# Reordering the first loads of an attention and MLP kernel: x tile 1 moves to the SP queue ahead of the keys, and wq moves behind the Exp warm-up on ACT

## Chip, cores, metric

One core of a Trainium2 chip. The metric is the device time of one execution in microseconds (us). A profile is one execution of its kernel, and its span is about 1.8 us shorter than the measured time of the same execution.

## The reference, cut to what matters

```python
x = A_x                                  # 2048 x 512, bf16
xn = _layernorm(x, axis=-1)
q = heads(xn @ wq)                       # 32 heads of 128
p = softmax(einsum("bhqd,bhkd->bhqk", q, k_cache) * 128 ** -0.5)
s = (p @ v_cache, heads side by side) @ wo
g = silu(relu(xn @ w1 + b1) ** 2 @ w2 + b2)
return x + s * g
```

(Condensed.) The projections start from xn, so no query and no score can be computed before the first tile of x is in SBUF.

## The kernel before

It is tuned: 4 query blocks of 512 rows, 32 heads each, with TensorE (PE) fed without a gap once it runs. Only the start matters here. Block 0 is brought in as four x tiles of 128 rows ("tile 0" to "tile 3"). Head 0's keys come in two halves and are transposed on PE. In the traces each engine works its list in program order (PE before the change: keys 4.86, tile 0 at 5.71, keys 5.95, projection 6.72 us). The loads are issued as below (SP and ACT each have a queue; a load without an engine goes to SP):

```python
    ln_load(0, 0, SP)          # x tile 0
    ln_load(0, 1, AC)          # x tile 1, on ACT's queue
    load_k0(0)                 # head 0's keys, first half
    fill_wq(0, AC)             # head 0's columns of wq, on ACT's queue
    load_k0(1)                 # head 0's keys, second half
    E(AC, partial(_act, out=th_t[:, 0, 0:1], in_=warm[:, 0:1], func=ACT.Exp), deps=[t_warm])
    ln_load(0, 2, SP)
    ln_load(0, 3, SP)
    fill_wq(1)
    load_v0(0)
    load_v0(1)
    # ... cut ...
```

And the work that waits for them, in the order in which PE and VectorE (DVE) get it:

```python
    warm_up(36)                # 36 dummy products, to bring PE to full clock (products 107 ns apart, then 56)
    k0_transpose(0)            # PE: keys, first half     (needs the load of that half)
    k0_copy(0)                 # ACT
    ln_bn(0, 0)                # DVE: statistics of tile 0
    ln_rstd(0, 0, eng=DV)      # DVE, GpSimd
    ln_bn(0, 1)                # DVE: statistics of tile 1 -- ahead of the next line on DVE
    ln_scale(0, 0)             # DVE: xn of tile 0
    first_transpose(0)         # PE
    k0_transpose(1)            # PE: keys, second half
    k0_copy(1)                 # ACT
    # ... cut ...
    first_copy(0)              # DVE
    first_proj(0)              # PE: head 0's queries of tile 0 (needs wq)
    # ... cut ...
    first_evac(0)
    first_transpose(1)
    gen_scores(0)              # PE: "the first scores"
```

The softmax here doesn't subtract the row's maximum and nothing guards it: scores larger than these inputs give would overflow.

## Time and profile before

| | before |
|---|---|
| time | 1238.17 us median of 3 runs (1237.9 to 1238.31) |
| PE busy | 99% of the span of 1236.1 us |
| tile 0 landed | 3.43 us |
| first projection starts on PE | 6.72 us |
| first scores start on PE | 7.58 us |

A load counts as landed when the last of its 16 semaphore increments is recorded. Those times come from the trace's records of increments, and the other two from the chain of waits, whose columns are start, length and what it was. The prediction shows that chain up to the projection. Here is the line after it:

```profile
7.58 1.05 PE psA L157 x16
```

From here on PE (TensorE) works without a gap worth the name.

### The profile page before, as it was taken

What the parts mean: (1) busy time and instruction counts of PE and PEld (TensorE: products, weight loads), DVE (VectorE), ACT (ScalarE), POOL (GpSimd) and SP (SyncE); (2) the same over time, 40 slices, a digit from 0 to 9 for tenths busy, and PEclk for the clock granted to TensorE, in tenths of its full rate; (3) what the DMA queues carried; (4) which work ended last, traced back from release to release, by engine and by line L of the source; (5) the groups of instructions that cost most, each with busy time, mean ns of one, the idle gap of its engine ahead of it and who ended that gap; (6) DMA issues with size and microseconds to landing.
All of it is one profiled execution on the core that took longest, in us unless ns stands there. A gap on an engine that the chain in (4) does not pass through costs nothing.

```text
span 1236.1 us, 26728 instructions
## 1 busy us (share of the span) xinstructions
PE 1220.8 (99%) x11678; PEld 819.1 (66%) x11885; DVE 472.8 (38%) x953; ACT 1054.6 (85%) x1044; POOL 32.0 (3%) x73
## 2 busy tenths in 40 slices
PE   9999999999999999999999999999999999999998
PEld 7666666666666666666666666666666666666665
DVE  4453323244435332334444532333344333324333
ACT  7888888888888888888888888888888888888885
POOL 1010000000002000000000200000000000000000
PEclk9999999999999999999999999999999999999999
DMA  9999998787879897768779878787778788878771
GB/s 211 203 245 194 187 178 134 130 144 143 140 152 171 144 158 129 141 138 144 133 135 169 171 138 144 141 148 133 134 146 148 146 154 158 137 134 146 145 124 31
DMA packets 686868, 185.41 MB, mean 150 GB/s; under 512 B 673536, under 2 KB 685568, under 8 KB 686752
## 3 DMA queue, kind: packets, MB, share of 16 engines
q1 hardware_dynamic: 684656, 179.62, 80.0%
q0 software_dynamic: 1424, 3.81, 1.2%
q8 instruction: 94, 1.54, 0.6%
q10 hardware_dynamic: 672, 0.26, 0.1%
q14 instruction: 22, 0.18, 0.0%
HBM read 96.60 MB, written 2.10 MB: 80 GB/s over the span
## 4 chain that ended last, share of the span: by engine, by line
PE 98%; issue 1%; DVE 0%; DMA 0%; POOL 0%; DVEq 0%
PE psO L157 38%; PE psA L152 35%; PE psF L152 25%; PE psA L157 0%; DMA x_ln<-in_A_x_dram 0%; DVE out_t L165 0%; PE psF L196 0%; DVE tmp_t L175 0%; PE psO L152 0%; DVE xnT L179 0%; DVE st_t L200 0%; POOL rstd L165 0%; DVE xn_t L171 0%; DVE mv_t L204 0%; DVE ve_t L171 0%
## 5 line engine op out<-in xcount | busy, mean ns | idle before, releaser
L161 ACT ACTIVATE pT<-psA 128x1024 bf16<-128x1024 f32 x1024 | 1044.5, 1024 | 162.9 <-PE psA L152 117.6
L157 PEld LDWEIGHTS psO<-v_sb,pT 128*128 128x128 bf16 x8192 | 547.9, 98 | 240.3 <-issue 12.4
L157 PE MATMUL psO<-v_sb,pT 128*128 128x129 bf16 x8192 | 631.2, 220 | 0.5
L152 PE MATMUL psA<-qt_sb,kT 128*128 128x512 bf16 x1840 | 562.9, 379 | 10.1
L179 DVE COPY o_un<-psO 128x258 f32<-128x258 f32 x256 | 97.4, 422 | 399.5 <-PE psO L157 398.8
L152 PE MATMUL psF<-xnT,wq_sb 128*128 128x512 bf16 (+1 forms) x508 | 165.7, 374 | 0.4 <-DVE xnT L179 0.2
L152 PE MATMUL psF<-wo_all,oT 128*128 128x512 bf16 x478 | 163.2, 379 | 0.1
L152 PEld LDWEIGHTS psA<-qt_sb,kT 128*128 128x128 bf16 x2032 | 157.0, 98 | 0.0
L179 DVE CAST qt_sb<-psF 128x512 bf16<-128x512 f32 (+1 forms) x130 | 88.0, 677 | 97.3 <-PE psF L152 93.7
L165 DVE TENSOR_TENSOR o_bf<-o_un,rden 128x512 bf16<-128x512 f32 x128 | 88.6, 692 | 4.7 <-DVE rden L183 0.3
L152 PEld LDWEIGHTS psF<-xnT,wq_sb 128*128 128x128 bf16 x520 | 50.3, 98 | 60.0 <-issue 0.3
L171 DVE TENSOR_SCALAR r_t<-psF,b1f 128x512 bf16<-128x512 f32 x56 | 42.0, 750 | 117.4 <-PE psF L152 117.4
L152 PEld LDWEIGHTS psF<-wo_all,oT 128*128 128x128 bf16 x480 | 46.9, 98 | 56.4
L152 PE MATMUL psF<-xnT,w_sb 128*128 128x512 bf16 x224 | 77.1, 379 | 0.0
L152 PE MATMUL psF<-w_sb,h2T 128*128 128x512 bf16 x223 | 73.7, 379 | 0.0
L152 PEld LDWEIGHTS psF<-xnT,w_sb 128*128 128x128 bf16 x224 | 21.9, 98 | 26.4
L152 PEld LDWEIGHTS psF<-w_sb,h2T 128*128 128x128 bf16 x224 | 21.9, 98 | 26.4
L165 DVE TENSOR_TENSOR z_t<-psF,b2bc 128x512 f32<-128x512 f32 x16 | 11.1, 692 | 67.2 <-PE psF L152 62.0
L165 DVE TENSOR_TENSOR acc<-psF,acc 128x512 f32<-128x512 f32 x28 | 19.3, 689 | 30.0 <-PE psF L152 30.0
L208 POOL DMA_DIRECT2D out_dram<-out_t x12 | 6.7, 554 | 891.1 <-DVE out_t L165 891.1
L165 DVE TENSOR_TENSOR h2T<-r_t 128x512 bf16<-128x512 bf16 x56 | 23.8, 426 | 1.9
L183 DVE RECIPROCAL rden<-o_un 128x4 f32<-128x4 f32 x128 | 22.9, 179 | 4.4
(47 smaller groups left out, 165.2 us busy)
## 6 DMA issues: line engine op xcount, KB each, us to landing
v_sb<-in_A_v_cache_dram SPq DMA_DIRECT2D x127, 512.0 KB, 4.7
wq_sb<-in_A_wq_dram SPq DMA_DIRECT2D x127, 128.0 KB, 3.1
wo_all<-in_A_wo_dram SPq DMA_DIRECT2D x4, 1024.0 KB, 6.4
w_sb<-in_B_w_dram SPq DMA_DIRECT2D x14, 256.0 KB, 4.1
oT<-o_bf SPq DMA_TRANSPOSE x128, 4.0
x_t<-in_A_x_dram POOLq DMA_DIRECT2D x16, 128.0 KB, 3.5
kT<-in_A_k_cache_dram SPq DMA_TRANSPOSE x127, 4.5
x_ln<-in_A_x_dram SPq DMA_DIRECT2D x15, 128.0 KB, 4.0
```

What stands on the lines that cost most here:

```text
L152: return e.matmul(out, lhsT, rhs, start=start, stop=stop)
L157: return e.matmul(out, lhsT, rhs, start=start, stop=stop, skip_group_check=True)
L161: return e.activation(out, in_, func, bias=bias, scale=scale)
L165: return e.tensor_tensor(out, in0, in1, op)
L171: return e.tensor_scalar(out, in0, scalar1=scalar1, scalar2=scalar2, op0=op0, op1=op1)
L179: return e.tensor_copy(out, in_)
L183: return e.reciprocal(out, in_)
L208: return e.dma_start(out, in_)
```

## The change

The intent: tile 0 should have the DMA engines to itself, since layernorm of tile 0 is at the head of the chain. So tile 1 stands behind it on SP, the keys behind both, and wq is alone on ACT's queue, behind Exp.

```diff
     ln_load(0, 0, SP)
-    ln_load(0, 1, AC)
+    ln_load(0, 1, SP)
     load_k0(0)
-    fill_wq(0, AC)
     load_k0(1)
     E(AC, partial(_act, out=th_t[:, 0, 0:1], in_=warm[:, 0:1], func=ACT.Exp), deps=[t_warm])
+    fill_wq(0, AC)
     ln_load(0, 2, SP)
```

## The prediction

> **What bounds the kernel now.** I read the page first (busy shares and the chain that ended last), then busy time by stage, then the chain of waits over the first 10 us, then the timeline of the same stretch with the DMA issues, and last the recorded increments of each load's semaphore. The page:
>
> ```profile
> span 1236.1 us, 26728 instructions
> PE 1220.8 (99%) x11678; PEld 819.1 (66%) x11885; DVE 472.8 (38%) x953; ACT 1054.6 (85%) x1044; POOL 32.0 (3%) x73
> ...
> PE 98%; issue 1%; DVE 0%; DMA 0%; POOL 0%; DVEq 0%
> ```
>
> TensorE (PE) is busy 99% of the span and is 98% of the chain that ended last. The change touches no instruction on PE; it reorders the loads at the start. So it can win only what PE loses there. Busy time by stage:
>
> ```profile
> 0.00:5.00 5.00, 4.02 (x38) 3.90 (x39) 1.48 (x4) 1.49 (x2) 1.83 (x12) 1.00 0.63 177
> 5.00:10.00 5.00, 4.61 (x70) 3.84 (x68) 4.06 (x14) 3.77 (x4) 2.20 (x5) 1.00 1.25 260
> 10.00:20.00 10.00, 9.87 (x140) 8.21 (x139) 3.83 (x13) 8.22 (x10) 1.34 (x3) 1.00 1.03 202
> ```
>
> The columns are stretch and length, then busy us on PE, PEld, DVE, ACT, POOL, then clock, DMA share and GB/s. From 10 us on PE is dense. The 4.02 us of PE work in the first stretch are the 36 dummy matmuls that warm it up, not real work, so the first real product waits on the chain that fills the first 7.6 us:
>
> ```profile
> 0.72 2.71 DMA x_ln<-in_A_x_dram
> ...
> 3.45 0.71 DVE st_t L200
> ...
> 4.64 0.58 POOL rstd L165
> ...
> 5.25 0.42 DVE xn_t L171
> ...
> 5.71 0.41 PE psF L196 x4
> ...
> 6.15 0.44 DVE xnT L179
> ...
> 6.72 0.38 PE psF L152 x4
> ```
>
> This is layernorm of x tile 0, its transpose on PE at 5.71, the copy, and head 0's first projection at 6.72. The chain starts with the landing of tile 0: issued at 0.72, landed at 3.43. From landing to the PE transpose is 5.71 - 3.43 = 2.28 us of fixed work on DVE and POOL. The loads and the transposes of head 0's keys stand around it:
>
> ```profile
> 0.72 0.41 ACTq L208 DMA_DIRECT2D x_ln<-in_A_x_dram  x1
> 0.72 0.40 SPq L208 DMA_DIRECT2D x_ln<-in_A_x_dram  x1
> ...
> 1.16 0.46 ACTq L208 DMA_DIRECT2D wq_sb<-in_A_wq_dram  x1
> 1.18 0.89 SPq L208 DMA_DIRECT2D kT<-in_A_k_cache_dram  x2
> ...
> 1.65 1.28 ACT L161 ACT_TABLE_LOAD   x1 [1.65 <-PEq L1024]
> ...
> 4.86 0.73 PE L196 MATMUL psO<-ident,kT 128*128 128x128 bf16 x8
> ...
> 5.89 0.49 PEld L196 LDWEIGHTS psO<-ident,kT 128*128 128x128 bf16 x8
> ```
>
> The semaphore records say when each landed: tile 0 3.43, tile 1 3.60, first half of the keys 4.82, head 0's wq 5.19, second half of the keys 5.85, tiles 2 and 3 at 6.23 and 6.64, head 1's wq 7.24, the two halves of the values 8.44 and 9.51. PE takes its work in program order: keys half one (4.86, 0.04 us after its landing, and just after the last dummy matmul at 4.69), x tile 0's transpose, keys half two (5.89, 0.04 us after its landing), first projection. Three things therefore stand within 0.3 us of one another on PE: tile 0 and the two halves of the keys.
>
> **What the Trainium skill says.** "DMA: Bandwidth & Descriptors", section "Issuing engines are not separate DMA queues": loads from SP and ACT end on the same 16 DMA engines and interleave; a second issuer saves issue time only. The trace agrees: both x tiles are issued at 0.72 and land 0.17 us apart. Same page, "Queues, rings and completion order": within one engine descriptors of one ring start in order, and an engine alternates between rings packet by packet. The trace agrees: from 2.4 to 2.6 us, 34 packets of SP's ring and 26 of ACT's began, and no key packet (behind tile 0 on SP's ring) before 2.6. "Advanced Engine Details and Errata", section "Sequencer Loop": engine instructions are pushed into a queue, and the sequencer goes on to control instructions. If it holds for a DMA issue behind an ACTIVATE, wq is issued at once; no record of the kernel before shows that order on ACT. "ScalarE: Activation LUTs", section "What ACT_TABLE_LOAD costs", gives about 1283 ns for a table load; the trace has 1.28 us.
>
> **The change part by part.** It adds and removes no instruction; it moves two DMA issues.
>
> 1. Tile 1 moves from ACT's ring to SP's, behind tile 0. Tile 0 then has the DMA engines to itself until something else comes on ACT's ring. A 1 KB packet took 46 ns (median), and a tile has 128 over 16 engines, so tile 1 is 8 x 46 = 0.37 us of each engine, mostly interleaved with tile 0 now. Part of the stretch up to 2.4 us is slow start, which stays. I expect tile 0 to land 0.2 to 0.35 us earlier, about 3.15. Tile 1 is second, so it lands near where it did (both are the first 256 KB in either order), about 3.6; DVE wants it only at 4.47, or 4.2 when shifted.
>
> 2. SP has one more issue (0.40 us plus a 0.06 us gap) ahead of the keys, so all its later issues come 0.46 us later. Keys half one is issued at 1.64 instead of 1.18. But it was not waiting for its issue: it was issued at 1.18 and its first packet ran at 2.6, and from 2.4 us on the DMA engines are about 90% busy. The same bytes (both tiles, wq, keys) lie ahead of each landing as before, only reordered, so I estimate 4.7 to 4.95 for half one and 5.8 to 6.0 for half two. Later landings gain up to 0.46 us, against slacks of 1 us or more: head 1's wq 7.24 for use at 8.64, values 9.51 for use at 11.52, and head 1's keys 12.75 for use at about 15.7. Nothing new there.
>
> 3. wq now stands behind the Exp warm-up on ACT. If the sequencer passes the queued Exp, it issues at about 0.8 to 1.0; if it waits for the table load and the Exp (1.28 + 0.21 us after about 0.75), at about 2.3. With the 4.0 us it took from issue to landing it is there at about 5.0 or 6.3, for a projection at 6.69 now and about 6.5 after. Early, its 256 B packets (18 ns each, 32 per engine, 0.58 us) compete with tile 0 and take some of point 1 back: eight alternations cost tile 0 up to 8 x 18 = 0.14 us. Late, they compete with the keys.
>
> The sum on PE: keys half one can start no earlier than about 4.78 (end of the dummies), takes eight issues in 0.57 us and ends at 5.35 to 5.55. Tile 0's transpose is ready at 3.15 + 2.28 = 5.43, so it starts at about 5.45 to 5.6 instead of 5.71. Keys half two (0.50 us) follows its landing: 5.85 + 0.04 + 0.50 = 6.39 at best, against xnT ready at 5.5 + 0.98 = 6.48. So the first projection starts at about 6.5 instead of 6.69. The gain is 0.1 to 0.3 us, I take 0.2, and PE carries it to the end as it is dense from there. 1238.17 - 0.2 = 1237.97, say 1238.0. In per cent it is 0.02, below the spread of the three runs of before (0.41 us).
>
> **The rivals.** (a) Keys take the place of tile 0: half one is issued 0.46 us later and lands that much later, at 5.28; then its transposes end at 5.9 and tile 0's transpose starts 0.15 to 0.2 us later than before. For it: PE was released by that landing at 4.86, with no slack. Against it: busy DMA engines from 2.4 us. It would make 1238.3 to 1238.5. (b) wq becomes the last to come: issued behind table load and Exp, landing after 6.7. For it: 4.0 us to landing; against it: its ring would be free, while before it stood behind tile 1. 0 to 0.3 us lost, so up to 1238.5. (c) The full intent: tile 0 0.4 us earlier and the keys unharmed, 1237.8. PE's own order and the second half of the keys stand against more. (d) Anything of 2% (25 us) would need PE to stop in the body, where the order of loads is untouched and SP waits for PE anyway. I see no way.
>
> **Range and chances.** All cases lie within 0.5 us of 1238.0; the runs of before spread over 0.4 us, and another build or another hour may add as much. So 1237.3 to 1238.8. Within 2% is all but certain.
>
> **What would show it.** In the changed trace: tile 0's landing near 3.15 with DVE's first statistics right behind; the keys' first landing below 4.95; the transpose of x tile 0 at 5.45 to 5.6; head 0's first projection near 6.5; and the same dense PE after that. A wq issue on ACT at 0.8 to 1.0 or at about 2.3 decides point 3. The prediction is wrong if the first projection starts later than 6.7, or if PE's idle after 10 us changes by more than some tenths of a us.

## More of the kernel before

I read each increment as the share of one of the core's 16 DMA engines. That is an assumption: the records show 16 increments per load and do not name the engine.

## The result, and the profile after

The changed kernel took 1238.44 us (median of 6, 1238.1 to 1239.05) against 1238.02 us (6 runs, 1237.9 to 1238.31). The ratio is 1.0004, interval 0.9991 to 1.0017: the same. Executions over 1.5% slower than the fastest of the same kernel are left out of the means. Ratios here are over the same rounds; they agree with the ratio of the mean times within 0.0001. In means, the changed kernel is 0.46 us slower (1238.51 against 1238.05). That is inside the reported interval (a second set of rounds, no. 2, gave 0.48 again), but the trace can say where it came from. The page of the changed kernel:

```profile
span 1236.5 us, 26935 instructions
PE 1231.8 (100%) x11885; PEld 819.3 (66%) x11885; DVE 472.3 (38%) x953; ACT 1053.7 (85%) x1044; POOL 32.0 (3%) x73
...
PE 99%; DMA 0%; DVE 0%; SPq 0%; issue 0%; DVEq 0%
```

PE busy seems to rise by 11 us. It did not: before, the page counted 11678 products beside 11885 weight loads, so 207 records of products were missing; after, none is. PEld, with all its records, has 819.1 and 819.3 us.

Busy time by stage (columns as in the prediction: stretch, length, busy PE, PEld, DVE, ACT, POOL, clock, DMA share, GB/s):

```profile
0.00:5.00 5.00, 4.02 (x36) 3.76 (x36) 1.77 (x5) 1.49 (x2) 2.04 (x12) 1.00 0.61 173
5.00:10.00 5.00, 4.32 (x63) 3.83 (x63) 3.28 (x12) 3.43 (x4) 1.98 (x4) 1.00 1.07 219
10.00:20.00 10.00, 9.93 (x145) 8.44 (x143) 3.90 (x12) 8.30 (x9) 1.34 (x3) 1.00 1.04 198
```

From 0 to 5 us PE lost its two key transposes (38 products before, 36 now); from 5 to 10 us the DMA rate fell from 260 to 219 GB/s and PE did 63 products in place of 70. The chain of waits at the start is another one now:

```profile
2.11 4.50 DMA kT<-in_A_k_cache_dram
...
6.66 0.62 PE psO L196 x8
7.28 0.24 PE psF L152 x4
...
7.98 1.05 PE psA L157 x16
```

It no longer begins with tile 0. It begins with the second half of the keys, issued at 2.11 and landed at 6.61 (ahead of it the view has only SP's three earlier issues, from 0.72). PE transposes it at 6.66, then projects, and the first scores start at 7.98, not 7.58: 0.40 us later, and the span is 0.4 us longer. The timeline of the same stretch (start, length, engine, line, operation):

```profile
0.72 1.28 ACT L161 ACT_TABLE_LOAD   x1 [0.72 <-PEq L1024]
0.72 0.87 SPq L208 DMA_DIRECT2D x_ln<-in_A_x_dram  x2
...
0.96 0.41 ACTq L208 DMA_DIRECT2D wq_sb<-in_A_wq_dram  x1
...
1.65 0.90 SPq L208 DMA_DIRECT2D kT<-in_A_k_cache_dram  x2
...
3.08 0.69 DVE L200 BATCH_NORM_STATS2 st_t<-x_ln 128x6 f32<-128x512 bf16 x1 [3.08 <-DMA x_ln<-in_A_x_dram]
...
5.96 0.40 PE L196 MATMUL psF<-ident,xn_t 128*128 128x128 bf16 x4
```

Tile 0 is in at 3.05 and DVE starts at 3.08, 0.37 us earlier than before: the change did what it was meant to. But the transpose of tile 0 on PE starts at 5.96, 0.25 us *later* than before, because the keys stand ahead of it on PE and half one landed at 5.09 (and its transposes ran at half speed, see no. 4). wq was issued at 0.96 and landed at 3.56, 1.63 us earlier than before and some 3.5 us before the projection wants it.

### The profile page after: what moved, and what is told of

Its sections match the earlier page's. It is cut to its first block, busy times and chain, and to the rows that moved or that the text cites. A ratio compares the mean times of both kernels' runs of the same rounds, so it can differ in the third digit from the quotient of the medians.

```text
span 1236.5 us, 26935 instructions
## 1 busy us (share of the span) xinstructions
PE 1231.8 (100%) x11885; PEld 819.3 (66%) x11885; DVE 472.3 (38%) x953; ACT 1053.7 (85%) x1044; POOL 32.0 (3%) x73
## 4 chain that ended last, share of the span: by engine, by line
PE 99%; DMA 0%; DVE 0%; SPq 0%; issue 0%; DVEq 0%
PE psO L157 38%; PE psA L152 36%; PE psF L152 25%; DMA kT<-in_A_k_cache_dram 0%; PE psA L157 0%; DVE out_t L165 0%; SPq L208 0%; DVE tmp_t L175 0%; PE psO L152 0%; PE psF L196 0%; PE psO L196 0%; DVE xnT L179 0%; DVE qt_sb L179 0%; DVEq L119 0%
## 5 line engine op out<-in xcount | busy, mean ns | idle before, releaser
L152 PE MATMUL psA<-qt_sb,kT 128*128 128x512 bf16 x2032 | 604.4, 379 | 0.0
L152 PE MATMUL psF<-xnT,wq_sb 128*128 128x512 bf16 (+1 forms) x520 | 168.8, 374 | 0.1
```

The costliest lines, as they stand in the source:

```text
L152: return e.matmul(out, lhsT, rhs, start=start, stop=stop)
```

## The experiments

Eleven experiments ran, two of them on the same two kernels again; all were correct. Only in nos. 3 and 8 does the 95% interval exclude a ratio of 1. So differences of some tenths of a us rest on the traces and on repetition. The rounds of nos. 1 to 4, 5 to 8 and 9 to 11 ran on three different chips, each with the kernel before beside it. Landings of the profiled execution, in us (for keys half two: the first, the 8th and the last of the 16 increments):

| kernel | tile 0 | tile 1 | wq | half one | half two first / 8th / last | first scores | span less first scores | mean time less before's, same rounds |
|---|---|---|---|---|---|---|---|---|
| before | 3.43 | 3.60 | 5.19 | 4.82 | 5.02 / 5.36 / 5.85 | 7.58 | 1228.5 | |
| before, again | 3.44 | 3.62 | 5.53 | 5.15 | 5.22 / 5.54 / 6.21 | 7.60 | 1228.5 | one run |
| changed | 3.05 | 3.89 | 3.56 | 5.09 | 4.90 / 5.45 / 6.61 | 7.98 | 1228.5 | +0.46 |
| changed, again | 2.90 | 4.02 | 3.64 | 5.35 | 4.92 / 5.86 / 7.35 | 8.72 | 1228.5 | +0.48 |
| tile 1 behind wq | 2.96 | 5.72 | 3.74 | 4.48 | 5.11 / 5.31 / 5.90 | 8.68 | 1228.5 | +2.15 |
| 40 dummies | 2.98 | 3.87 | 3.56 | 4.93 | 5.05 / 5.35 / 6.59 | 7.96 | 1228.5 | +0.49 |
| Exp order only | 3.40 | 3.58 | 5.72 | 4.49 | 5.13 / 5.31 / 6.41 | 7.78 | 1228.5 | -0.06 |
| keys, then tile 1 | 2.93 | 6.17 | 4.44 | 5.07 | 4.48 / 5.05 / 5.79 | 9.62 | 1228.9 | +1.71 |
| wq after tile 0 | 2.89 | 3.27 | 7.71 | 4.86 | 4.54 / 4.73 / 5.51 | 8.63 | 1228.5 | +1.19 |
| tiles 2, 3 on ACT | 2.92 | 4.08 | 3.69 | 6.23 | 5.71 / 6.56 / 7.53 | 9.23 | 1229.3 | +2.53 |
| tile 1 only | 3.28 | 4.09 | 3.74 | 5.36 | 4.98 / 5.87 / 6.72 | 8.09 | 1228.5 | +0.23 |
| half two behind projection | 2.87 | 4.00 | 3.65 | 5.44 | 4.88 / 5.52 / 7.55 | 8.27 | 1229.0 | +0.57 |
| wq after ident | 2.87 | 3.34 | 6.49 | 5.22 | 5.09 / 5.60 / 6.32 | 7.69 | 1228.5 | +0.13 |

Read the column "span less first scores" first. In ten of thirteen profiles it is 1228.5 us, whatever the loads did. So all the time that these ten win or lose is won or lost before the first scores. The three others have a second loss after it, told below.

This gives an estimate for the runs that were not profiled. A time is the first scores, plus 1228.5, plus the 1.8 us by which it exceeds the span. By that the 33 timed runs of the kernel before had their first scores at 7.55 to 8.52, median 7.8, and the 11 of the changed kernel at 7.8 to 8.75, median 8.25. So the two profiles of before, at 7.58 and 7.60, are among its quickest executions, and 20 of its 33 runs lose 0.1 us or more against these; the profile of no. 11 is its kernel's quickest of five, those of nos. 6 and 10 are among the slowest of theirs. A row of landings is one draw.

**1. The kernel before, a second profile.** No edit.

> The kernel before, unchanged, for a second profile. Slot theory (the keys land when their place in SP's order lets them): landings repeat within 0.1 us of the first profile, keys half one 4.82, half two 5.85, head 0's first projection 6.72. Chance theory (the slowest of the 16 DMA engines sets each landing and differs from run to run): one of the two moves by more than 0.2 us, and with it the first projection.

Both halves of the keys came 0.33 to 0.36 us later than in the first profile, yet the projection started at 6.74 against 6.72 and the time was 1237.91. So the landings of the keys do vary by chance; but in these two executions the kernel before doesn't care, because tile 0's chain, which repeats within 0.02 us, sets the projection. It was close: the transposes of half two ended at about 6.7 in the second, so keys later than that would have delayed it (no. 5 shows a case). The slot theory fails as stated, and the chance theory is half right.

**2. The changed kernel, a second profile and five more times.** No edit.

> The changed kernel, unchanged, for a second profile and more times. Slot theory: tile 0 lands at 3.05, keys half one at 5.09 and half two at 6.61 again, within 0.1 us; first scores at 7.98; time 0.4 us over before. Chance theory: the keys' landings move by more than 0.2 us in either direction, first scores anywhere from 7.4 to 8.0, and the mean time lies 0 to 0.3 us over before.

1238.57 us (1238.14 to 1239.04) against 1238.01 (9 runs, 1237.88 to 1238.29), ratio 1.0003. The chain of waits of this execution, the slowest but one of the eleven timed:

```profile
2.11 5.24 DMA kT<-in_A_k_cache_dram
...
8.72 1.05 PE psA L157 x16
```

Half two landed at 7.35 this time, and its first scores are 0.74 us later than in the first profile. The time of that execution is 1239.04 against 1238.29 of the first: 0.75 us more. So in the changed kernel PE's wait at the start ends with a load whose landing varies, and the time takes over its variation; in the two profiles of before that load had slack. Neither theory foresaw a landing as late as this; the mean loss is over what the chance theory allowed.

**3. Tile 1 on ACT's queue, behind wq.** The keys get their old slots on SP.

```diff
     ln_load(0, 0, SP)
-    ln_load(0, 1, SP)
     load_k0(0)
     ...
     fill_wq(0, AC)
+    ln_load(0, 1, AC)
```

> Tile 1 goes to ACT's queue behind wq, so the keys have their old place on SP (issued at 1.18 and 1.65) and tile 0 still has no other x tile beside it. Slot theory: keys half one lands at 4.4 to 4.8, half two at 5.5 to 5.9, tile 0 at 3.05 to 3.15, first scores at 7.3 to 7.4, time 0.1 to 0.3 us under before. Chance theory: keys land as in the changed kernel, 5.0 or later in this profile or another, and the time is within 0.15 us of the changed kernel's.

1240.13 us (1239.01 to 1241.69), ratio 1.0017, interval 1.0005 to 1.003: slower than both, by less than 2%. The keys did land as the slot theory said (4.48 and 5.90), and tile 0 at 2.96. But:

```profile
1.45 4.27 DMA x_ln<-in_A_x_dram
...
5.75 0.69 DVE st_t L200
...
8.68 1.05 PE psA L157 x16
```

The chain now starts with tile 1, issued at 1.45 and landed at 5.72: its 1 KB packets ran from 3.56 to 5.26, among the 2 KB packets of the keys (2.83 to 5.39). DVE has the statistics of tile 1 ahead of the scaling of tile 0 in its program, so tile 0, in since 2.96, waits. This is the same fault as in the change, with another load: what comes early stands in line behind what comes late.

**4. 40 dummy products in place of 36**, on the changed kernel.

```diff
-    warm_up(36)
+    warm_up(40)
```

> The changed kernel with 40 dummy products in place of 36, to bridge TensorE to 5.2 us so that it isn't idle when the keys land. Cold-clock theory (the idle from 4.8 to 5.14 us kept TensorE at 107 ns a product through the first eight transposes): the eight key transposes start near 5.23 and run at 56 ns after about 5.15, so tile 0's transpose starts at about 5.7 and not 5.96; first scores 0.15 to 0.25 us earlier unless half two of the keys is as late as 6.6, in which case they gain nothing. Rival, that the clock steps up at a fixed time whatever runs: the eight transposes stay at 107 ns until 5.9, and tile 0's transpose starts at 6.05 or later.

1238.54 us (1238.15 to 1238.92), as the changed kernel in the same rounds (1238.57). PE was never idle from 0.98 to 5.98 us, and still the eight key transposes ran at 107 ns each, from 5.23 to 5.97. So the cold-clock theory falls: idling did not hold the clock down. The rival, a fixed time, forecast this profile (tile 0's transpose came at 6.08), but falls as well when all profiles are compared. The first pair of products 56 ns apart came at 3.83 us in the second profile of before, at 5.15 in the first, and after 5.97 here, though PE began at 0.98 in all of them. When the clock steps up differs from profile to profile, and nothing here says why; with half two at 6.59 it made no difference.

**5. Exp's place alone.** The order of before, with wq behind Exp.

```diff
     ln_load(0, 1, AC)
     load_k0(0)
-    fill_wq(0, AC)
     load_k0(1)
     E(AC, ... Exp ...)
+    fill_wq(0, AC)
```

> One part of the change alone: Exp moves ahead of ACT's loads, tile 1 stays on ACT ahead of wq, SP's order is that of before. ACT's loads should be issued near 0.96 and 1.42 (before: 0.72 and 1.16). If the loss comes from the keys and SP's order, this kernel is within 0.1 us of before in the mean, first scores at 7.4 to 7.6, keys landing by 5.2 and 6.3. If Exp ahead of ACT's loads were the cause, it shows the 0.3 to 0.4 us loss of the changed kernel.

1238.08 us (1237.88 to 1238.12) against 1238.11 (9 runs): nothing, ratio 1.0. My text had the order on ACT wrong: Exp stands between tile 1 and wq, as in the change, and the issues were at 0.72 and 1.23 (I had expected 0.96 and 1.42). The profiled execution had half two at 6.41, for its last increment alone (the one before came at 5.86), and first scores at 7.78; it is the slowest of the five. So before's order, too, can lose 0.2 us in this way now and then.

**6. Keys first, tile 1 behind them on SP.**

```diff
     ln_load(0, 0, SP)
-    ln_load(0, 1, SP)
     load_k0(0)
     load_k0(1)
+    ln_load(0, 1, SP)
```

> Keys in their old place on SP (issued at 1.18 and 1.65), tile 1 behind them on SP, wq alone on ACT as in the change, so that no second ring has work from about 3.1 us on. Tile 1 lands late (after 5.3) and DVE's order makes the whole 0.5 us or more slower, which isn't the question; the question is when the keys land. Slot theory (their place on SP decides): half one by 4.6, half two at 5.2 to 5.6, since 128 KB less lie ahead than in the changed kernel. Lone-ring theory (with only SP's ring active the key packets stall on single engines; with ACT's ring active beside it they don't): half two at 5.9 or later, its slowest engine 1 us or more behind its fastest, moved bytes under 300 GB/s from 3.2 to 4.8 us.

1239.89 us (4 runs), slower as expected since tile 1 landed at 6.17. Half two landed at 5.79, between the two forecasts, with a spread of 1.31 us and 295 and 310 GB/s in the two halves of 3.2 to 4.8 us: inconclusive. This profile also shows a second loss: PE was back at 107 ns for about half of the first 16 products of the scores (in no. 8 for 14 of them), where the eleven other profiles have 56. The granted clock, the third column from the end, shows what it was (this kernel first, then no. 8):

```profile
7.20:10.50 3.30, 3.19 (x29) 2.96 (x30) 2.29 (x8) 1.02 (x1) 1.25 (x2) 0.50 1.24 226
8.00:11.30 3.30, 3.25 (x32) 3.01 (x30) 1.30 (x4) 2.05 (x3) 0.74 (x2) 0.50 1.12 214
```

It had stepped up (products 56 ns apart from 3.73 and 4.55 us on) and fell back to half for these stretches; no other profile has one around its first scores. Why it fell back is not shown.

**7. wq only after tile 0 has landed.** SP keeps the order of the change.

```diff
     E(AC, ... Exp ...)
+    S.emit_wait(AC, [t_xl[0]])
     fill_wq(0, AC)
```

> The changed kernel, but ACT issues wq only when tile 0 has landed, so that wq's small packets stand beside the keys (as before the change) and not ahead of them. Tile 0 lands at 2.7 to 2.95, tile 1 at 3.2 to 3.5. Lone-ring theory, or simply fewer bytes ahead: keys half one at 4.2 to 4.6, half two at 5.6 to 6.0, wq at 5.3 to 6.0; first scores at 7.25 to 7.45, time 0.1 to 0.3 us under before. Slot theory: keys are no earlier than in the changed kernel less wq's 0.4 us, half two at 6.2 or later, first scores 7.5 to 7.8, time 0 to 0.3 us over before.

Half two landed at 5.51 with the keys' late slots on SP, 1.1 us earlier than in the changed kernel. That speaks against the slot theory, which had 6.2 or later: SP's extra issue ahead of the keys did not make them late here. What left their way is wq. But wq itself now came too late:

```profile
2.91 4.80 DMA wq_sb<-in_A_wq_dram
7.71 0.05 issue
7.76 0.41 PE psF L152 x4
```

1238.95 us (1238.84 to 1240.55). I had expected wq at 5.3 to 6.0; it landed at 7.71, and the scores came at 8.63 instead of 7.25 to 7.45; its first packet ran at 4.58, and its packets ran among those of SP's later loads.

**8. Tiles 2 and 3 on ACT behind wq**, to have a second ring at work beside the keys.

```diff
     fill_wq(0, AC)
-    ln_load(0, 2, SP)
-    ln_load(0, 3, SP)
+    ln_load(0, 2, AC)
+    ln_load(0, 3, AC)
```

> The changed kernel with x tiles 2 and 3 on ACT's queue behind wq: SP's slots for the keys are the late ones of the change, but a second ring has work while the keys move. Lone-ring theory: from 3.2 to 4.8 us over 310 GB/s, half two lands at 5.7 to 6.2 although 256 KB more go beside it, the time is at most 0.1 us over before. Slot theory: half two lands at 6.6 or later, with the two tiles' bytes added up to 7.3, and the time is 0.4 us or more over before.

1240.6 us (4 runs), ratio 1.0021, half two at 7.53, 262 and 230 GB/s in the two halves of 3.2 to 4.8 us. The lone-ring theory falls: with the second ring at work the keys were slower yet. (No. 7 speaks against it as well: no second ring was at work until 4.58 us, and half two was the earliest of all.) These two agree with a simple reading, that the keys are later the more bytes go ahead of them or beside them; the kernel before and the changed one have the same bytes and differ all the same.

**9. Tile 1's move alone**, wq ahead of Exp.

```diff
     ln_load(0, 0, SP)
     ln_load(0, 1, SP)
     load_k0(0)
+    fill_wq(0, AC)
     load_k0(1)
     E(AC, ... Exp ...)
-    fill_wq(0, AC)
```

> The other part of the change alone: tile 1 goes to SP ahead of the keys, wq stays ahead of Exp on ACT (issued at 0.72 in place of 0.96). Theory: the move of tile 1 leaves wq first on ACT's ring, wq's packets run ahead of the keys, and the last engines bring the second half of the keys after 6.2. Then this kernel is like the changed one: half two 6.3 to 7.4 with a spread over 1.3 us between its first and last engine, mean time 0.3 to 0.6 us over before. Rival, that it takes both moves: mean within 0.15 us of before.

1238.4 us (1238.07 to 1238.64) against 1238.1 (9 runs, one of them 1238.83), ratio 1.0002. Half two landed at 6.72, spread 1.74 us, as the theory said; the mean loss, 0.23 us, is a little under its 0.3 and over the rival's 0.15; it is within what the runs scatter. Together with no. 5: it is tile 1's move that makes half two late (it also leaves wq first on ACT's ring), and Exp's does not.

**10. Half two transposed behind the projection**, on the changed kernel.

```diff
     first_transpose(0)
-    k0_transpose(1)
-    k0_copy(1)
-    t_kfill[0] = t_k0[1]
     ...
     first_proj(0)
+    k0_transpose(1)
+    k0_copy(1)
+    t_kfill[0] = t_k0[1]
```

> The changed kernel, but TensorE transposes the second half of the keys behind head 0's first projection and not ahead of it. Theory: it is the wait for half two, in TensorE's order ahead of the projection, that eats tile 0's early landing. Then the first projection starts at 6.4 to 6.9 though half two still lands after 6.2, and the mean time is 0.1 to 0.4 us under the changed kernel's 1238.55 of the earlier rounds, that is 0 to 0.3 us over before. Rival (the projection waits for something else, or the loss is merely passed on to the scores of half two): mean within 0.1 us of the changed kernel's.

The projection started at 7.06, before half two was in (7.55), so that wait was gone. It was later than the 6.4 to 6.9 forecast, because half one came at 5.44 and stood ahead of tile 0 on PE. But 1238.91 us (1238.14 to 1239.06), 0.57 us over before: nothing won. The chain shows where it went:

```profile
2.11 5.43 DMA kT<-in_A_k_cache_dram
...
8.25 1.03 ACT kT L161
9.28 0.05 issue
9.33 0.62 PE psA L157 x8
```

The scores of half two had to wait for half two, its transposes and ACT's copy, and stand right behind the first. The rival was right: the loss is passed on (hence 1229.0 in the table). The second half of the keys is needed within 0.5 us of the first scores, wherever its transposes stand.

**11. wq after the identity matrix**, so that it is issued at 1.91.

```diff
     E(AC, ... Exp ...)
+    S.emit_wait(AC, [t_ident])
     fill_wq(0, AC)
```

> The changed kernel, but ACT issues wq only when GpSimd has made the identity matrix, about 1.9 us, so that wq's packets run at about 3.2 as before the change, beside the keys. Theory (wq ahead of the keys makes half two late): tile 0 lands at 2.75 to 2.95, tile 1 by 3.4, keys half one by 4.9, wq at 5.0 to 5.8, half two at 5.6 to 6.1; first projection at 6.35 to 6.7; mean time 0 to 0.3 us under before. Rival (it is tile 1 ahead of the keys on SP that makes them late, wherever wq runs): half two after 6.2 and mean 0.3 us or more over before.

1238.27 us (1238.03 to 1238.87), ratio 1.0001. wq's packets ran beside the keys again, as before the change. Half two landed at 6.32, later than the theory's 6.1 and later than the rival's 6.2, with a spread of 1.23 us:

```profile
2.11 4.21 DMA kT<-in_A_k_cache_dram
...
7.69 1.05 PE psA L157 x16
```

The first scores are at 7.69, 0.11 us later than before, and the mean loss was 0.13 us against 0.46 to 0.48 of the changed kernel. That suggests that wq running ahead of the keys is most of the loss. It does not prove it: the two means are of different rounds and chips, this profile is the quickest of its five runs (the slowest, 1238.87, is near the changed kernel's worst), and no. 9, with wq ahead, lost only 0.23 us in the same rounds. No version was clearly faster than the kernel before.

## Why the prediction was right or wrong

**The time fell in the range, the sign was wrong, and so was the path.** I put 1238.0 us with a range of 1237.3 to 1238.8, and all but certainty for "the same"; it was 1238.44. But the range was wide enough to hold the rivals as well, so this says little for the mechanism. I forecast a gain of 0.2 us, and the means show a loss of 0.46; and by my own sign ("wrong if the first projection starts later than 6.7") the account of the start was wrong: it started at 7.12. That the body of the kernel would not move was right to 0.1 us (span less first scores).

**Point 1, tile 0: right.** Forecast about 3.15, measured 3.05 and 2.90. Tile 1 was forecast near 3.6 and came at 3.89 and 4.02, with wq's packets now ahead of it (wq landed at 3.56); it cost little, as DVE took it up at 4.09 and 4.04. (Where the prediction says that the trace agrees with engines alternating packet by packet, the trace shows only packets of both rings in the same 0.2 us; its records do not name the engine.)

**Point 3, wq: the case was left open, its consequence missed.** wq was issued at 0.96, in the early case. I gave it 4.0 us to land, the time of the kernel before. That time held a wait behind tile 1 in ACT's own ring; with the ring free it took 2.6 us. So wq went ahead of the keys (494 of its 512 packets of 256 B began before the first packet of the keys; before, none did), where before it had run beside them. I charged its estimated 0.58 us on each engine to tile 0 alone.

**Point 2, the keys: the step that failed.** It said: "The same bytes (both tiles, wq, keys) lie ahead of each landing as before, only reordered, so I estimate 4.7 to 4.95 for half one and 5.8 to 6.0 for half two." Measured: 5.09 and 5.35, 6.61 and 7.35. The bytes were the same, and the middle of the load was little later: the 8th increment of half two came at 5.45 and 5.86 after, at 5.36 and 5.54 before. But a load has landed when the *last* of its 16 increments is in, and the spread between first and last went from 0.83 and 0.99 us to 1.71 and 2.43. In the five profiles in which wq and tile 1 both ran ahead of the keys and no other load was moved (changed, twice; 40 dummies; tile 1 only; half two behind projection), half two landed at 6.59 to 7.55. In the four with wq's packets beside the keys (before, twice; Exp order only; wq after ident) it was 5.85 to 6.41, and with wq behind them (wq after tile 0) 5.51. Where wq ran early but tile 1 did not run ahead of the keys (nos. 3 and 6), it was 5.90 and 5.79: wq's early start alone does not do it. Each is one execution, but the groups do not overlap.

**The rival that came true is (a), the keys taking the place of tile 0, at its size (1238.3 to 1238.5) but not for its reason.** It put the lateness down to SP's extra issue. No. 7 shows the keys at 5.51 with that issue in place. Its path, half one in front of tile 0 on PE, did come about (tile 0's transpose at 5.96 and 5.85, against its 5.86 to 5.91), but what the projection waited for was half two. With half two moved away (no. 10), the first path alone left the projection at 7.06.

**The sum on PE.** Forecast: projection at about 6.5. Measured: 7.12 and 7.86. (Two readings in the prediction are a little off, and nothing rests on them: the projection of before started at 6.72, 6.69 being its weight load, and the first packet of the keys ran at 2.73, not 2.6.) In the first profile the eight key transposes also ran at 107 ns, which helped to put tile 0's transpose at 5.96; no. 4 shows that this was not what held up the end.

**What stays open.** Why the last increments lag so much more when tile 1 and wq's small packets have both gone first. In the traces of before and changed I see longer single key packets (the longest 0.88 and 0.96 us changed, 0.50 and 0.58 before, the median 84 ns in all four profiles), and fewer bytes moved from 4.8 to 5.6 us (233 and 201 GB/s changed, 318 and 367 before). Neither is the mark of a late half two: no. 4 moved 322 GB/s in that stretch and no. 11 had a packet of 1.07 us, with half two at 6.59 and 6.32. Slot, lone ring and cold clock were tested and are out as sole causes, slot and lone ring by one or two profiles each; "bytes ahead of the keys" explains nos. 7 and 8 and not the spread at equal bytes.

## What to carry to other kernels

Making the first load of a chain land earlier is worth only the distance to the second-latest input that the in-order engine wants next; measure that distance first (here 0.3 us: half two was transposed by 6.4 and the projection started at 6.7, and the keys scatter by as much). Time a load by its last increment, not by bytes over bandwidth: with other loads moved ahead of the keys, their 8th increment came 0.1 to 0.3 us later and their last 0.8 to 1.1 us. And when a load is taken out of a queue, look at what moves up in its place: wq came 1.6 us earlier than before, although nobody wanted it sooner, and what was wanted came later.

## What the Trainium skill lacked or had wrong

- "TensorE: Matmul & The Clock Gate", section "What's actually happening", says that the clock steps up after about 3.4 us of sustained work, with the point varying by 500 ns, because the window in which the work is counted runs freely. A free-running window may well be the reason here too, but the 500 ns do not hold: it varied by far more. With dummies from 0.98 us on, the first products 56 ns apart came at 3.83 and 5.15 us in two profiles of the same kernel, and in no. 4 after 5.0 us of unbroken work (0.98 to 5.98) they were still 107 ns apart.
- "Advanced Engine Details and Errata", section "Sequencer Loop", has engine instructions pushed into a queue while control instructions are executed by the sequencer. It does not say on which side a DMA issue stands. Here it passed queued engine work (wq was issued at 0.96, in a table load from 0.72 to 2.01, ahead of the Exp at 2.02), but not always at once. Where the Exp ahead of it still lacked its semaphore (the memset that sets it ended at 0.92), the issue came 0.24 us after the table load's start; where the semaphore was there already (no. 5) it came 0.06 us after. From these two cases, an engine instruction's unmet wait seems to hold the issue behind it, while its execution does not.
- On no page that I read: how far the 16 increments of one load can drift apart. For the second half of the keys (256 KB) the last increment came 0.8 to 2.7 us after the first over the thirteen profiles, and it is this that decides when a wait ends.
